# Casting weight loads, a state load in 512-byte runs, and an interleaved start, in an attention + FFN kernel

## The chip, the cores and the metric

One core of one Trainium2 chip. The metric is the device time of one execution in microseconds (us). A profile's "span" is from the first to the last instruction and is about 2 us shorter than the time. Engines: PE (matrix multiply), DVE (VectorE), ACT (ScalarE), POOL (GpSimd), SP (SyncE, which here only issues DMAs). A DMA "lands" when its data has arrived. To "evict" is to copy a result of PE out of its accumulator. The "granted clock" is the share of the full TensorE clock that the profile gives PE. Run to run the kernel before stays within 0.5% of its median.

## The reference, cut to what matters

```python
# x: (8, 8, 512, 64), state: (8, 8, 32, 64)  = batch, head, row, dim; fp32
scores = softmax(x @ state.T / 8)          # per batch and head: 512 x 32
xread  = scores @ state                    # 512 x 64
scores2 = softmax(state @ x.T / 8)         # 32 x 512
sread  = scores2 @ x                       # 32 x 64
tokens = concat([xread, sread], rows)      # (8, 544, 512), heads side by side
out = leaky_relu(tokens @ w_in) @ w_out    # w_in 512 x 2048, w_out 2048 x 512
```

Both kernels never form xread: since xread is A @ state, they compute M = state @ w_in per batch (called M below) and then FFN1 as A @ M. FFN1 is the product with w_in, FFN2 that with w_out. The largest piece is FFN2, 512 matmuls of 128x512 for the x rows alone.

## The kernel before

The loads and the order of the start are what the argument touches. Weights go through a staging tile of two buffers and are cast by DVE:

```python
    def load_w_in(n):
        st = stage.tile([P, NK, 512], FP32, name="w_stage", tag="w_stage", bufs=2)
        nc.sync.dma_start(st[:], moe_w_in[:, 512 * n:512 * (n + 1)].rearrange("(k p) c -> p k c", p=P))
        nc.vector.tensor_copy(w_in_bf[n][:], st[:])
    # ... load_w_out likewise
    def load_state():                       # eight DMAs, runs of 64 fp32 = 256 bytes
        for k in range(NK):
            for g in range(2):
                nc.scalar.dma_start(
                    stf[32 * k:32 * (k + 1), :, 64 * g:64 * (g + 1)],
                    state[:, 2 * k + g, :, :].rearrange("b n d -> n b d"))
    # ... cuts
    load_state(); load_x(0); load_w_in(0); load_x(1); load_w_in(1); load_x(2)   # lines joined here
    load_w_in(2); load_w_in(3)
    for n in range(4):
        load_w_out(n)
    prep_state()
    for b in range(AHEAD):                  # AHEAD = 2
        cast_x(b); att_xT(b, 0); att_xT(b, 1)
        att_scores(b); att_sread(b); att_aT(b)
    cast_x(2)
    for n in range(4):
        for b in range(AHEAD):
            m_chunk(b, n)
            for j in range(4 * n, 4 * n + 4):
                ffn1(b, j)
        # ... attention and M of batch 2
    for b in range(B):                      # steady state: FFN2 of b, FFN1 of b+2, attention of b+3
        # ...
```

The softmax here doesn't subtract the row's maximum and nothing guards it: scores larger than these inputs give would overflow.

Of the kernel before, what the change touches and what calls it, by code (L numbers as in the profile page):

```python
# [25 lines left out]
def kernel(  # L26
# [34 lines left out]
    stf = consts.tile([P, B, P], FP32, name="stf")  # L61
# [14 lines left out]

    def load_state():
        for k in range(NK):
            for g in range(2):
                nc.scalar.dma_start(  # L80
                    stf[32 * k:32 * (k + 1), :, 64 * g:64 * (g + 1)],
                    state[:, 2 * k + g, :, :].rearrange("b n d -> n b d"))

    def prep_state():
        for half in range(2):
            b0 = 4 * half
            nc.vector.tensor_copy(stb[:, b0:b0 + 4, :], stf[:, b0:b0 + 4, :])  # L87
            pst = psum.tile([P, 4, P], BF16, name="pst", tag="big")
            for i in range(4):
                nc.tensor.transpose(pst[:, i, :], stb[:, b0 + i, :], ident[:])  # L90
            for g in range(2):
                nc.vector.tensor_copy(  # L92
                    bd[64 * g:64 * (g + 1), b0:b0 + 4, :, g, :],
                    pst[64 * g:64 * (g + 1), :, :].rearrange("p b (k n) -> p b k n", k=NK),
                )

    def load_x(b):
        st = bt[b]
        st.xf = stage.tile([P, H, 4 * D], FP32, name="xf", tag="xf")
        nc.sync.dma_start(st.xf[:], x[b].rearrange("h (p t) d -> p h (t d)", t=4))  # L100

    def cast_x(b):
        st = bt[b]
        st.xb = attw.tile([P, 4, H, D], BF16, name="xb", tag="xb")
        for hh in range(2):
            src = st.xf[:, 4 * hh:4 * hh + 4, :].rearrange("p h (t d) -> p t h d", t=4)
            nc.gpsimd.tensor_copy(st.xb[:, :, 4 * hh:4 * hh + 4, :], src)  # L107

    def load_w_in(n):
        st = stage.tile([P, NK, 512], FP32, name="w_stage", tag="w_stage", bufs=2)  # L110
        nc.sync.dma_start(
            st[:], moe_w_in[:, 512 * n:512 * (n + 1)].rearrange("(k p) c -> p k c", p=P))
        nc.vector.tensor_copy(w_in_bf[n][:], st[:])

    def load_w_out(n):
        st = stage.tile([P, 4, DM], FP32, name="w_stage", tag="w_stage", bufs=2)
        nc.sync.dma_start(
            st[:], moe_w_out[512 * n:512 * (n + 1), :].rearrange("(j p) c -> p j c", p=P))
        nc.vector.tensor_copy(w_out_bf[n][:], st[:])


    def att_xT(b, half):
        st = bt[b]
        if half == 0:
            st.pxt = psum.tile([P, NK, 4, P], BF16, name="pxt", tag="big")
            st.xT = attw.tile([P, NK, 4, P], BF16, name="xT", tag="xT")
        for k in (2 * half, 2 * half + 1):
# [5 lines left out]
        if half == 1:  # L133
            nc.vector.tensor_copy(st.xT[:], st.pxt[:])  # L134

    def att_scores(b):
        st = bt[b]
        sc = psum.tile([P, 4, 2, NK, NS], FP32, name="sc", tag="big")
        for t in range(4):
            for k in range(NK):  # L140
                nc.tensor.matmul(  # L141
                    sc[:, t, :, k, :], lhsT=st.xT[:, k, t, :], rhs=bd[:, b, k, :, :],
                    start=True, stop=True)
        st.E = attw.tile([P, 4, 2, NK, NS], BF16, name="E", tag="E")
        nc.scalar.activation(out=st.E[:], in_=sc[:], func=ACTF.Exp, scale=SCALE)  # L145
        r1 = attw.tile([P, 32], FP32, name="r1", tag="r1")
        nc.vector.tensor_reduce(
            out=r1[:], in_=st.E[:].rearrange("p t g k n -> p (t g k) n"),
            op=ALU.add, axis=mybir.AxisListType.X)
        rr1 = attw.tile([P, 32], FP32, name="rr1", tag="rr1")  # L150
        nc.vector.reciprocal(rr1[:], r1[:])
        st.A = attw.tile([P, 4, 2, P], BF16, name="A", tag="A")
        nc.vector.tensor_tensor(  # L153
            out=st.A[:].rearrange("p t g (k n) -> p (t g k) n", n=NS),
            in0=st.E[:].rearrange("p t g k n -> p (t g k) n"),
            in1=rr1[:, :, None].to_broadcast([P, 32, NS]), op=ALU.mult)
# [24 lines left out]
    def att_aT(b):  # L181
        st = bt[b]
        pat = psum.tile([P, 2, 4, P], BF16, name="pat", tag="big")
        for g in range(2):
            for t in range(4):
                nc.tensor.transpose(pat[:, g, t, :], st.A[:, t, g, :], ident[:])  # L186
        st.aT = fpool.tile([P, 2, 4 * P], BF16, name="aT", tag="aT")
        nc.vector.tensor_copy(st.aT[:], pat[:].rearrange("p g t q -> p g (t q)"))  # L188


    def m_chunk(b, n):
# [10 lines left out]
        st.M[n] = fpool.tile([P, 2, 512], BF16, name=f"M{n}", tag=f"M{n}", bufs=2)  # L202
        nc.vector.tensor_copy(st.M[n][:], pm[:])
# [5 lines left out]
    def ffn1(b, j):  # L209
# [5 lines left out]
        for g in range(2):  # L215
            nc.tensor.matmul(  # L216
                ph[:], lhsT=st.M[n][:, g, P * jj:P * (jj + 1)], rhs=st.aT[:, g, :],
# [44 lines left out]
    load_state()  # L262
    load_x(0)
    load_w_in(0)
    load_x(1)
    load_w_in(1)
    load_x(2)
    load_w_in(2)
    load_w_in(3)
    for n in range(4):  # L270
        load_w_out(n)

    prep_state()
    for b in range(AHEAD):
        cast_x(b)
        att_xT(b, 0)
        att_xT(b, 1)
        att_scores(b)
# [80 lines left out]
```

## Time and profile before

| | before |
|---|---|
| time, median of 3 runs | 270.09 us (269.61 to 270.3) |
| span of the profile | 267.9 us |
| first FFN1 matmul | 47.8 us |
| first FFN2 matmul | 65.8 us |
| last matmul ends | 264.2 us |

The page of the kernel before: busy tenths in 40 slices of 6.7 us for PE and for the DMA engines, the GB/s moved per slice, and what was read from HBM.

```profile
PE   0015264999999999999999999999999999999994
...
DMA  7998999500023111111111111111111111122322
GB/s 212 324 348 300 337 379 364 166 0 2 1 76 123 42 39 42 39 39 57 49 48 47 39 42 39 42 39 39 42 39 39 42 39 39 42 78 80 78 81 78
...
HBM read 17.30 MB, written 8.91 MB: 98 GB/s over the span
```

PE has seven slices with little work and is then full to the end; the DMA engines are the opposite. The windows view cut at the first FFN1 and the first FFN2 gives the busy us (and instruction counts) of PE, PEld (weight load), DVE, ACT and POOL, then the granted PE clock, the DMA share and GB/s:

```profile
0.00:47.80 47.80, 13.66 (x153) 11.16 (x154) 24.61 (x34) 3.33 (x3) 10.94 (x15) 1.00 0.98 324
47.80:65.80 18.00, 17.92 (x97) 6.07 (x98) 7.22 (x6) 12.75 (x23) 0.00 (x0) 1.00 0.14 45
65.80:264.20 198.40, 197.69 (x1394) 96.37 (x1392) 91.26 (x107) 72.25 (x128) 8.55 (x8) 1.00 0.14 50
```

PE works 13.7 of the first 47.8 us and 215.6 of the 216.4 us after. So for a change that leaves PE's work as it is, the start is the only place to win time. The timeline of the kernel before (start, duration, engine, line, operation, what it waited for in brackets) shows why the start is long:

```profile
0.74 9.66 ACTq L80 DMA_DIRECT2D stf<-in_state_dram  x8
...
17.62 1.23 DVE L113 CAST w_in_bf_90<-w_stage 128x2048 bf16<-128x2048 f32 x1 [6.31 <-DMA w_stage<-in_moe_w_in_dram]
18.76 0.76 DVE L87 CAST stb<-stf 128x512 bf16<-128x512 f32 x2
...
30.86 1.23 DVE L119 CAST w_out_bf_93<-w_stage 128x2048 bf16<-128x2048 f32 x1 [1.18 <-DMA w_stage<-in_moe_w_out_dram]
32.01 1.22 DVE L153 TENSOR_TENSOR A<-E,rr_196 128x1024 bf16<-128x1024 bf16 x1
...
47.79 0.61 PE L216 MATMUL ph<-aT,M_339 128*128 128x512 bf16 x1 [0.51 <-DVE M_339 L203]
```

The ACT queue issues the state loads from 0.74 us for 9.66 us. The cast of state starts only at 18.76 us, behind a weight cast in DVE's order, and A, the normalised scores, stands behind the cast of a w_out chunk. A 1 MB weight chunk takes 7.7 to 9.9 us in the median from issue to landing, queued behind others, and a 64 KB piece of state 7.9 us.

### The profile page before, as it was taken

How to read it: one execution, taken by the hardware profiler on the slowest of the kernel's cores; microseconds unless marked ns; L12 is line 12 of the kernel's file. 1: busy time of each engine (PE TensorE's matmuls, PEld its weight loads, DVE VectorE, ACT ScalarE, POOL GpSimd, SP SyncE). 2: the span in 40 equal slices, each digit the busy share in tenths (PEclk: the TensorE clock that was granted, in tenths of full speed). 3: DMA queues.
4: the chain of work that ended last, by engine and by line, in shares of the span. 5: the costliest groups of instructions: out<-in, count | busy, mean ns of one | idle time of the engine just before them, and what ended most of it. 6: DMA issues, size and time to landing. Idle time of an engine off the chain costs nothing.

```text
span 267.9 us, 3811 instructions
## 1 busy us (share of the span) xinstructions
PE 229.3 (86%) x1640; PEld 113.6 (42%) x1640; DVE 123.8 (46%) x147; ACT 88.3 (33%) x153; POOL 19.5 (7%) x23
## 2 busy tenths in 40 slices
PE   0015264999999999999999999999999999999994
PEld 0014253224446435543554455455445555444441
DVE  0136869633787854745375456546542111222111
ACT  0101010577625333543443353434344444200000
POOL 3230303000030200300030000000000000000000
PEclk9999999999999999999999999999999999999999
DMA  7998999500023111111111111111111111122322
GB/s 212 324 348 300 337 379 364 166 0 2 1 76 123 42 39 42 39 39 57 49 48 47 39 42 39 42 39 39 42 39 39 42 39 39 42 78 80 78 81 78
DMA packets 19729, 26.46 MB, mean 99 GB/s; under 512 B 3073, under 2 KB 11265, under 8 KB 19713
## 3 DMA queue, kind: packets, MB, share of 16 engines
q1 hardware_dynamic: 17536, 25.69, 27.9%
q10 hardware_dynamic: 2176, 0.52, 0.9%
q8 instruction: 13, 0.21, 0.3%
q14 instruction: 4, 0.02, 0.0%
HBM read 17.30 MB, written 8.91 MB: 98 GB/s over the span
## 4 chain that ended last, share of the span: by engine, by line
PE 79%; DVE 9%; DMA 8%; ACT 1%; issue 1%; DVEq 0%; ACTq 0%
PE py L240 40%; PE ph L216 21%; PE pm L199 4%; DMA w_stage<-in_moe_w_in_dram 4%; PE pxt L129 3%; PE phs L225 3%; PE pys L252 3%; DMA xf<-in_x_dram 2%; DMA w_stage<-in_moe_w_out_dram 2%; DVE A L153 2%; PE pat L186 2%; PE sc L141 1%; ACT E L145 1%; DVE xT L134 1%; PE pr L168 1%; PE pr L162 1%
## 5 line engine op out<-in xcount | busy, mean ns | idle before, releaser
L207 ACT ACTIVATE hT<-ph 128x512 bf16<-128x512 f32 x128 | 75.0, 597 | 104.2 <-PE ph L216 104.2
L240 PEld LDWEIGHTS <-hT 128*128 128x128 bf16 x512 | 47.1, 98 | 51.6 <-issue 5.2
L245 DVE COPY ysb<-py 128x512 f32<-128x512 f32 x32 | 22.1, 692 | 61.2 <-PE py L240 61.2
L240 PE MATMUL py<-w_out_bf_95,hT 128*128 128x512 bf16 x128 | 33.5, 381 | 0.0
L240 PE MATMUL py<-w_out_bf_94,hT 128*128 128x512 bf16 x128 | 33.2, 380 | 0.0
L240 PE MATMUL py<-w_out_bf_93,hT 128*128 128x512 bf16 x128 | 33.2, 380 | 0.0
L240 PE MATMUL py<-w_out_bf_96,hT 128*128 128x512 bf16 x128 | 32.9, 380 | 0.0
L107 POOL CAST xb<-xf 128x1024 bf16<-128x1024 f32 x16 | 17.0, 1092 | 118.7 <-issue 55.2
L90 PE MATMUL pst<-ident,stb 128*128 128x128 bf16 x8 | 1.0, 311 | 19.2 <-DVE stb L87 19.2
L145 ACT ACTIVATE E<-sc 128x1024 bf16<-128x1024 f32 x8 | 8.2, 1023 | 27.2 <-PE sc L141 27.2
L134 DVE COPY xT<-pxt 128x2048 bf16<-128x2048 bf16 x8 | 9.8, 1225 | 15.3 <-PE pxt L129 15.3
L186 PE MATMUL pat<-ident,A 128*128 128x128 bf16 x64 | 5.7, 243 | 8.9 <-DVE A L153 8.9
L129 PE MATMUL pxt<-ident,xb 128*128 128x128 bf16 x128 | 12.1, 242 | 0.7 <-DVE bd L92 0.7
L129 PEld LDWEIGHTS <-xb 128*128 128x128 bf16 x128 | 9.9, 110 | 4.7 <-issue 1.4
L199 PEld LDWEIGHTS <-bd 64*32 64x32 bf16 x256 | 4.5, 90 | 16.8 <-issue 15.0
L186 PEld LDWEIGHTS <-A 128*128 128x128 bf16 x64 | 4.6, 108 | 10.6 <-DVE A L153 9.7
L90 PEld LDWEIGHTS <-stb 128*128 128x128 bf16 x8 | 0.8, 136 | 19.2 <-DVE stb L87 19.2
L188 DVE COPY aT<-pat 128x1024 bf16<-128x1024 bf16 x8 | 5.5, 682 | 7.2 <-PE pat L186 7.2
L141 PE MATMUL sc<-bd,xT 128*128 128x64 bf16 x128 | 5.8, 205 | 2.6 <-DVE xT L134 2.6
L162 PE MATMUL pr<-E,osel 128*128 128x128 bf16 x64 | 5.8, 241 | 2.3 <-ACT E L145 2.2
L141 PEld LDWEIGHTS <-xT 128*128 128x128 bf16 x128 | 5.2, 106 | 4.7 <-DVE xT L134 3.8
L162 PEld LDWEIGHTS <-osel 128*128 128x128 bf16 x64 | 5.0, 108 | 4.3 <-issue 2.8
(178 smaller groups left out, 254.2 us busy)
## 6 DMA issues: line engine op xcount, KB each, us to landing
xf<-in_x_dram SPq DMA_DIRECT2D x8, 1024.0 KB, 9.1
out_dram<-ysb SPq DMA_DIRECT2D x32, 256.0 KB, 2.3
w_stage<-in_moe_w_in_dram SPq DMA_DIRECT2D x4, 1024.0 KB, 9.9
w_stage<-in_moe_w_out_dram SPq DMA_DIRECT2D x4, 1024.0 KB, 7.7
stf<-in_state_dram ACTq DMA_DIRECT2D x8, 64.0 KB, 7.9
out_dram<-ysb SPq DMA_DIRECT2D x8, 64.0 KB, 1.7
```

Source lines behind the costliest of these rows:

```text
L107: nc.gpsimd.tensor_copy(st.xb[:, :, 4 * hh:4 * hh + 4, :], src)
L129: nc.tensor.transpose(st.pxt[:, k, t, :], st.xb[:, t, 2 * k:2 * k + 2, :].rearrange("p h d -> p (h d)"), ident[:])
L134: nc.vector.tensor_copy(st.xT[:], st.pxt[:])
L141: nc.tensor.matmul(sc[:, t, :, k, :], lhsT=st.xT[:, k, t, :], rhs=bd[:, b, k, :, :], start=True, stop=True)
L145: nc.scalar.activation(out=st.E[:], in_=sc[:], func=ACTF.Exp, scale=SCALE)
L162: nc.tensor.matmul(pr[:, 1, 0, :], lhsT=osel[:, g, :], rhs=st.E[:, t, g, :, :].rearrange("p k n -> p (k n)"), start=(i == 0), stop=(i == 7))
L186: nc.tensor.transpose(pat[:, g, t, :], st.A[:, t, g, :], ident[:])
L199: nc.tensor.matmul(pm[32 * k:32 * (k + 1), g, :], lhsT=bd[sl, b, k, g, :], rhs=w_in_bf[n][sl, k, :], start=True, stop=True)
L207: nc.scalar.activation(out=dst, in_=src, func=ACTF.Prelu, alpha=0.01)
L216: nc.tensor.matmul(ph[:], lhsT=st.M[n][:, g, P * jj:P * (jj + 1)], rhs=st.aT[:, g, :], start=(g == 0), stop=(g == 1))
L240: nc.tensor.matmul(acc.py[:], lhsT=st.hT[:, j, P * t:P * (t + 1)], rhs=w_out_bf[j // 4][:, j % 4, :], start=(j == 0), stop=(j == 15))
L245: nc.vector.tensor_copy(ysb[:], acc.py[:])
```

## The change

Its intent: take weight casts and staging off DVE by DMAs that cast while they move; load state in one DMA with runs of 512 bytes; and start FFN1 of batch 0 as soon as that batch is through attention, with everything else interleaved behind it. The Trainium skill, page "DMA: Bandwidth & Descriptors", section "SWDGE vs HWDGE vs iDMA", says that a DMA that casts has to be issued from GpSimd; that is why weights, and with them x of batches 1 and 2, move to that queue. The core of the diff:

```diff
 # weights: staging tile and VectorE cast replaced by a DMA that casts
     def load_w_in(n):
-        st = stage.tile([P, NK, 512], FP32, name="w_stage", tag="w_stage", bufs=2)
-        nc.sync.dma_start(
-            st[:], moe_w_in[:, 512 * n:512 * (n + 1)].rearrange("(k p) c -> p k c", p=P))
-        nc.vector.tensor_copy(w_in_bf[n][:], st[:])
+        nc.gpsimd.dma_start(
+            w_in_bf[n][:], moe_w_in[:, 512 * n:512 * (n + 1)].rearrange("(k p) c -> p k c", p=P))
 # ... load_w_out likewise

 # state: one load; a partition holds 512 contiguous bytes (two rows of one head) per batch
     def load_state():
-        for k in range(NK):
-            for g in range(2):
-                nc.scalar.dma_start(
-                    stf[32 * k:32 * (k + 1), :, 64 * g:64 * (g + 1)],
-                    state[:, 2 * k + g, :, :].rearrange("b n d -> n b d"))
+        stf = stage.tile([P, B, P], FP32, name="stf", tag="xf")
+        nc.sync.dma_start(
+            stf[:], state.rearrange("b h n d -> b (h n d)").rearrange("b (p c) -> p b c", p=P))
+        return stf
 # ... prep_state: 8 transposes become 32 small matmuls with columns of the identity

 # order of work (cut)
-    load_state()
-    load_x(0)
+    load_x(0, parts=2)
+    stf = load_state()
     load_w_in(0)
-    load_x(1)
+    load_x(1, nc.gpsimd)
     load_w_in(1)
-    load_x(2)
     load_w_in(2)
     load_w_in(3)
+    load_x(2, nc.gpsimd)
     for n in range(4):
         load_w_out(n)
-    prep_state()
-    for b in range(AHEAD):          # all of attention of 0 and 1 ...
-        cast_x(b)
-        att_xT(b, 0)
-        att_xT(b, 1)
-        att_scores(b)
-        att_sread(b)
-        att_aT(b)
-    # ... and only then state @ w_in (m_chunk) and FFN1 of 0 and 1
+    cast_x(0, ("dve", "act", "dve", "act"))
+    att_xT(0, 0, "dve")
+    att_xT(0, 1, "act")
+    prep_state(stf, 0, ("dve", "dve", "act"))
+    att_scores(0)
+    att_softmax(0, 2)
+    prep_state(stf, 1, ("dve", "dve", "act"))
+    m_early(0, 0, ("act", "act"))
+    att_aT(0, ("dve", "act"))
+    cast_x(1, ("dve", "act"))
+    m_early(1, 0, ("act", "act"))
+    att_xT(1, 0, "dve")
+    att_xT(1, 1, "dve")
+    m_early(0, 1, ("dve", "act"))
+    for j in range(4):
+        ffn1(0, j)
+    att_scores(1)
+    # ... FFN1 of 0 and 1 in groups of four, between them m_early of 0, 1 and 2,
+    #     attention of 1 and 2, and at the end att_sread(0) and att_sread(1)
```

Not shown in the cut: a first activation that loads ACT's table early, casts and copies spread over DVE and ACT, x of batch 0 in two halves, and more buffers for some tiles.

More of the change, by code (lines that the diff above doesn't have):

```diff
@@ L59 @@
     nc.gpsimd.memset(bd[:], 0.0)
-    stf = consts.tile([P, B, P], FP32, name="stf")
     stb = consts.tile([P, B, P], BF16, name="stb")
@@ L74 @@
     bt = [Batch() for _ in range(B)]
-    def load_state():
-        for k in range(NK):
-            for g in range(2):
-                nc.scalar.dma_start(
-                    stf[32 * k:32 * (k + 1), :, 64 * g:64 * (g + 1)],
-                    state[:, 2 * k + g, :, :].rearrange("b n d -> n b d"))
-    def prep_state():
-        for half in range(2):
-            b0 = 4 * half
-            nc.vector.tensor_copy(stb[:, b0:b0 + 4, :], stf[:, b0:b0 + 4, :])
-            pst = psum.tile([P, 4, P], BF16, name="pst", tag="big")
-            for i in range(4):
-                nc.tensor.transpose(pst[:, i, :], stb[:, b0 + i, :], ident[:])
-            for g in range(2):
-                nc.vector.tensor_copy(
-                    bd[64 * g:64 * (g + 1), b0:b0 + 4, :, g, :],
-                    pst[64 * g:64 * (g + 1), :, :].rearrange("p b (k n) -> p b k n", k=NK),
-                )
@@ L97, in load_x, with copy, prep_state @@
-    def load_x(b):
+    def copy(eng, dst, src):
+        if eng == "act":
+            nc.scalar.copy(dst, src)
+        elif eng == "pool":
+            nc.gpsimd.tensor_copy(dst, src)
+        else:
+            nc.vector.tensor_copy(dst, src)
+    def load_state():
+        stf = stage.tile([P, B, P], FP32, name="stf", tag="xf")
+        nc.sync.dma_start(
+            stf[:], state.rearrange("b h n d -> b (h n d)").rearrange("b (p c) -> p b c", p=P))
+        return stf
+    def prep_state(stf, half, engs):
+        bs = slice(4 * half, 4 * half + 4)
+        copy(engs[0], stb[:, bs, :], stf[:, bs, :])
+        pst = psum.tile([P, 4, NK, NS // 2, 2], FP32, name="pst", tag="ph")
+        sel = ident[:].rearrange("p (k g n) -> p k g n", k=NK, g=2)
+        for i in range(4):
+            for g in range(2):
+                for r in range(2):
+                    nc.tensor.matmul(
+                        pst[64 * g:64 * (g + 1), i, :, :, r],
+                        lhsT=stb[:, 4 * half + i, 64 * r:64 * (r + 1)], rhs=sel[:, :, g, :],
+                        start=True, stop=True)
+        for g in range(2):
+            sl = slice(64 * g, 64 * (g + 1))
+            copy(engs[1 + g], bd[sl, bs, :, g, :],
+                 pst[sl].rearrange("p b k n r -> p b k (n r)"))
@@ L98, in load_x @@
+    def load_x(b, eng=None, parts=1):
         st = bt[b]
         st.xf = stage.tile([P, H, 4 * D], FP32, name="xf", tag="xf")
-        nc.sync.dma_start(st.xf[:], x[b].rearrange("h (p t) d -> p h (t d)", t=4))
-    def cast_x(b):
-        st = bt[b]
-        st.xb = attw.tile([P, 4, H, D], BF16, name="xb", tag="xb")
-        for hh in range(2):
-            src = st.xf[:, 4 * hh:4 * hh + 4, :].rearrange("p h (t d) -> p t h d", t=4)
-            nc.gpsimd.tensor_copy(st.xb[:, :, 4 * hh:4 * hh + 4, :], src)
+        src = x[b].rearrange("h (p t) d -> p h (t d)", t=4)
+        w = H // parts
+        for i in range(parts):
+            hs = slice(w * i, w * (i + 1))
+            (eng or nc.sync).dma_start(st.xf[:, hs, :], src[:, hs, :])
@@ L109, in load_w_in, with cast_x @@
+    def cast_x(b, engs=("pool", "pool")):
+        st = bt[b]
+        st.xb = attw.tile([P, 4, H, D], BF16, name="xb", tag="xb", bufs=4)
+        w = H // len(engs)
+        for i, eng in enumerate(engs):
+            src = st.xf[:, w * i:w * (i + 1), :].rearrange("p h (t d) -> p t h d", t=4)
+            copy(eng, st.xb[:, :, w * i:w * (i + 1), :], src)
     def load_w_in(n):
-        st = stage.tile([P, NK, 512], FP32, name="w_stage", tag="w_stage", bufs=2)
-        nc.sync.dma_start(
-            st[:], moe_w_in[:, 512 * n:512 * (n + 1)].rearrange("(k p) c -> p k c", p=P))
@@ L113, in load_w_in @@
-        nc.vector.tensor_copy(w_in_bf[n][:], st[:])
+        nc.gpsimd.dma_start(
+            w_in_bf[n][:], moe_w_in[:, 512 * n:512 * (n + 1)].rearrange("(k p) c -> p k c", p=P))
     def load_w_out(n):
-        st = stage.tile([P, 4, DM], FP32, name="w_stage", tag="w_stage", bufs=2)
-        nc.sync.dma_start(
-            st[:], moe_w_out[512 * n:512 * (n + 1), :].rearrange("(j p) c -> p j c", p=P))
-        nc.vector.tensor_copy(w_out_bf[n][:], st[:])
-    def att_xT(b, half):
+        nc.gpsimd.dma_start(
+            w_out_bf[n][:], moe_w_out[512 * n:512 * (n + 1), :].rearrange("(j p) c -> p j c", p=P))
@@ L123, in att_xT @@
+    def att_xT(b, half, eng="dve"):
         st = bt[b]
@@ L126, in att_xT @@
             st.xT = attw.tile([P, NK, 4, P], BF16, name="xT", tag="xT")
+        ks = slice(2 * half, 2 * half + 2)
         for k in (2 * half, 2 * half + 1):
@@ L132, in att_xT @@
                     ident[:])
-        if half == 1:
-            nc.vector.tensor_copy(st.xT[:], st.pxt[:])
+        copy(eng, st.xT[:, ks, :, :], st.pxt[:, ks, :, :])
     def att_scores(b):
         st = bt[b]
-        sc = psum.tile([P, 4, 2, NK, NS], FP32, name="sc", tag="big")
+        st.sc = psum.tile([P, 4, 2, NK, NS], FP32, name="sc", tag="big")
         for t in range(4):
@@ L141, in att_scores, with att_softmax @@
                 nc.tensor.matmul(
-                    sc[:, t, :, k, :], lhsT=st.xT[:, k, t, :], rhs=bd[:, b, k, :, :],
+                    st.sc[:, t, :, k, :], lhsT=st.xT[:, k, t, :], rhs=bd[:, b, k, :, :],
                     start=True, stop=True)
-        st.E = attw.tile([P, 4, 2, NK, NS], BF16, name="E", tag="E")
-        nc.scalar.activation(out=st.E[:], in_=sc[:], func=ACTF.Exp, scale=SCALE)
-        r1 = attw.tile([P, 32], FP32, name="r1", tag="r1")
-        nc.vector.tensor_reduce(
-            out=r1[:], in_=st.E[:].rearrange("p t g k n -> p (t g k) n"),
-            op=ALU.add, axis=mybir.AxisListType.X)
-        rr1 = attw.tile([P, 32], FP32, name="rr1", tag="rr1")
-        nc.vector.reciprocal(rr1[:], r1[:])
-        st.A = attw.tile([P, 4, 2, P], BF16, name="A", tag="A")
-        nc.vector.tensor_tensor(
-            out=st.A[:].rearrange("p t g (k n) -> p (t g k) n", n=NS),
-            in0=st.E[:].rearrange("p t g k n -> p (t g k) n"),
-            in1=rr1[:, :, None].to_broadcast([P, 32, NS]), op=ALU.mult)
+    def att_softmax(b, parts=1):
+        st = bt[b]
+        st.E = attw.tile([P, 4, 2, NK, NS], BF16, name="E", tag="E", bufs=3)
+        st.A = attw.tile([P, 4, 2, P], BF16, name="A", tag="A")
+        r1 = attw.tile([P, 4, 8], FP32, name="r1", tag="r1")
+        rr1 = attw.tile([P, 4, 8], FP32, name="rr1", tag="rr1")
+        w = 4 // parts
+        for i in range(parts):
+            ts = slice(w * i, w * (i + 1))
+            nc.scalar.activation(out=st.E[:, ts], in_=st.sc[:, ts], func=ACTF.Exp, scale=SCALE)
+        for i in range(parts):
+            ts = slice(w * i, w * (i + 1))
+            Ev = st.E[:, ts].rearrange("p t g k n -> p (t g k) n")
+            rv = rr1[:, ts].rearrange("p t c -> p (t c)")
+            nc.vector.tensor_reduce(
+                out=r1[:, ts].rearrange("p t c -> p (t c)"), in_=Ev,
+                op=ALU.add, axis=mybir.AxisListType.X)
+            nc.vector.reciprocal(rv, r1[:, ts].rearrange("p t c -> p (t c)"))
+            nc.vector.tensor_tensor(
+                out=st.A[:, ts].rearrange("p t g (k n) -> p (t g k) n", n=NS),
+                in0=Ev, in1=rv[:, :, None].to_broadcast([P, 8 * w, NS]), op=ALU.mult)
     def att_sread(b):
@@ L179, in att_sread, with att_aT @@
                 in1=rr2[sl, :].rearrange("p (k n) -> p k n", n=NS), op=ALU.mult)
-    def att_aT(b):
+    def att_aT(b, engs=("dve",)):
         st = bt[b]
         pat = psum.tile([P, 2, 4, P], BF16, name="pat", tag="big")
-        for g in range(2):
-            for t in range(4):
-                nc.tensor.transpose(pat[:, g, t, :], st.A[:, t, g, :], ident[:])
-        st.aT = fpool.tile([P, 2, 4 * P], BF16, name="aT", tag="aT")
-        nc.vector.tensor_copy(st.aT[:], pat[:].rearrange("p g t q -> p g (t q)"))
+        st.aT = fpool.tile([P, 2, 4, P], BF16, name="aT", tag="aT")
+        w = 4 // len(engs)
+        for i, eng in enumerate(engs):
+            ts = slice(w * i, w * (i + 1))
+            for t in range(w * i, w * (i + 1)):
+                for g in range(2):
+                    nc.tensor.transpose(pat[:, g, t, :], st.A[:, t, g, :], ident[:])
+            copy(eng, st.aT[:, :, ts, :], pat[:, :, ts, :])
     def m_chunk(b, n):
@@ L201, in m_chunk, with m_early @@
                     rhs=w_in_bf[n][sl, k, :], start=True, stop=True)
-        st.M[n] = fpool.tile([P, 2, 512], BF16, name=f"M{n}", tag=f"M{n}", bufs=2)
-        nc.vector.tensor_copy(st.M[n][:], pm[:])
+        st.M[n] = fpool.tile([P, 2, 512], BF16, name=f"M{n}", tag=f"M{n}", bufs=3)
+        copy("dve", st.M[n][:], pm[:])
+    def m_early(b, n, engs=("act", "act")):
+        st = bt[b]
+        if n == 0:
+            st.M = [None] * 4
+        pm = [psum.tile([P, 512], FP32, name=f"pme{g}", tag="py") for g in range(2)]
+        for k in range(NK):
+            for g in range(2):
+                sl = slice(64 * g, 64 * (g + 1))
+                nc.tensor.matmul(
+                    pm[g][32 * k:32 * (k + 1), :], lhsT=bd[sl, b, k, g, :],
+                    rhs=w_in_bf[n][sl, k, :], start=True, stop=True)
+        st.M[n] = fpool.tile([P, 2, 512], BF16, name=f"M{n}", tag=f"M{n}", bufs=3)
+        for g in range(2):
+            copy(engs[g], st.M[n][:, g, :], pm[g][:])
     def lrelu(dst, src):
@@ L216, in ffn1 @@
             nc.tensor.matmul(
-                ph[:], lhsT=st.M[n][:, g, P * jj:P * (jj + 1)], rhs=st.aT[:, g, :],
+                ph[:], lhsT=st.M[n][:, g, P * jj:P * (jj + 1)], rhs=st.aT[:, g, :, :].rearrange("p t q -> p (t q)"),
                 start=(g == 0), stop=(g == 1))
@@ L259, in ffn2_s @@
             nc.sync.dma_start(out[r0:r0 + NS, :], ysb[NS * i:NS * (i + 1), :])
-    load_state()
-    load_x(0)
+    load_x(0, parts=2)
+    stf = load_state()
+    warm = consts.tile([P, 1], FP32, name="warm")
+    nc.vector.memset(warm[:], 0.0)
+    nc.scalar.activation(out=warm[:], in_=warm[:], func=ACTF.Exp)
     load_w_in(0)
-    load_x(1)
+    load_x(1, nc.gpsimd)
     load_w_in(1)
-    load_x(2)
     load_w_in(2)
     load_w_in(3)
+    load_x(2, nc.gpsimd)
     for n in range(4):
         load_w_out(n)
-    prep_state()
@@ L274 @@
-    for b in range(AHEAD):
-        cast_x(b)
-        att_xT(b, 0)
-        att_xT(b, 1)
-        att_scores(b)
-        att_sread(b)
-        att_aT(b)
-    cast_x(2)
-    for n in range(4):
-        for b in range(AHEAD):
-            m_chunk(b, n)
-            for j in range(4 * n, 4 * n + 4):
-                ffn1(b, j)
-        if n == 2:
-            att_xT(2, 0)
-            att_xT(2, 1)
-            att_scores(2)
-        if n == 3:
-            att_sread(2)
-            att_aT(2)
-            m_chunk(2, 0)
-            m_chunk(2, 1)
-            m_chunk(2, 2)
-            m_chunk(2, 3)
+    cast_x(0, ("dve", "act", "dve", "act"))
@@ new lines @@
+    att_xT(0, 0, "dve")
[14 more added lines that the diff above has]
+    att_scores(1)
+    att_softmax(1, 2)
+    m_early(2, 0, ("dve", "dve"))
@@ new lines @@
+    for j in range(4, 8):
+        ffn1(0, j)
+    m_early(1, 1, ("dve", "dve"))
+    m_early(0, 2, ("dve", "dve"))
+    for j in range(8, 12):
+        ffn1(0, j)
+    att_aT(1)
+    m_early(0, 3, ("dve", "dve"))
+    for j in range(12, 16):
+        ffn1(0, j)
+    cast_x(2, ("dve", "dve"))
+    m_early(2, 1, ("dve", "dve"))
+    for j in range(4):
+        ffn1(1, j)
+    att_xT(2, 0)
+    att_xT(2, 1)
+    m_early(1, 2, ("dve", "dve"))
+    for j in range(4, 8):
+        ffn1(1, j)
+    att_scores(2)
@@ L299 @@
+    att_softmax(2)
+    m_early(1, 3, ("dve", "dve"))
+    for j in range(8, 12):
+        ffn1(1, j)
+    att_sread(0)
+    m_early(2, 2, ("dve", "dve"))
+    att_aT(2)
+    for j in range(12, 16):
+        ffn1(1, j)
+    m_early(2, 3, ("dve", "dve"))
+    att_sread(1)
     for b in range(B):
@@ L308 @@
                 1: [lambda: att_xT(c, 1)],
-                3: [lambda: att_scores(c)],
+                3: [lambda: att_scores(c), lambda: att_softmax(c)],
                 5: [lambda: att_sread(c)],
+                2: [lambda: att_sread(2)] if b == 0 else [],
                 8: [lambda: att_aT(c)],
```

## The prediction

> **What bounds the kernel now.** The page's slices show two regimes: from about 48 us to the end the matmul engine (PE) is at 90% or more in every slice (granted clock 1.00), and the chain of waits is 79% PE. Before that PE does little: the timeline puts the first FFN1 matmul at 47.8 us and the first FFN2 matmul at 65.8 us, and the windows view gives PE 13.9 us of work in the first 48. In that front the DMA engines run at about 330 to 375 GB/s and the chain alternates between weight and x transfers (8 to 10 us for a queued 1 MB load) and VectorE (DVE), which has eight weight casts of 1.23 us in order before softmax steps. State is prepared only at 18.8 us, behind a cast that waited for w_in; A of batch 0 waits behind a cast of w_out (30.9 to 32.1 us).
>
> **What changes.** Removed: 9.8 us of DVE casts, staging waits, and state in 256-byte runs, issued on the ACT queue until 10.4 us. Added: weight loads as GpSimd DMAs that cast, batch 0 attention in smaller pieces over DVE and ACT, 32 small state matmuls for 8 transposes. Moved: FFN1 of batch 0 before attention of batches 1 and 2, sread of 0 and 1 behind it.
>
> **Cost.** PE work is hardly changed. From the first FFN1 to the last matmul the kernel before needs 216 us (47.8 to 264.2); the one after should need about 219, for attention of batch 1 and two sreads move into it (about 3 us net). So the gain is how much earlier dense PE work starts, less the stalls. I estimate x of batch 0 landed by 5.5 us, state by 7, scores at 12, softmax and aT by 17. In PE's order the first FFN1 stands behind a matmul on w_in chunk 1, which at 0.35 MB per us lands at 16 to 19 us. First FFN1: about 19 us, 29 earlier. Given back, estimated: x of batch 2 is behind all of w_in, while early loads of x 3 to 5 share the engines; it lands at 28 to 33 us, and its cast stands in DVE's order before M chunk 3 of batch 0, so PE stalls 2 to 5 us. Then DVE (M evictions at about 0.69 us per half, softmax) and ACT (0.60 us per FFN1 eviction) hold FFN1 back by 3 to 5 us. FFN2 starts near 48 us. Span near 19+219+7+4 (tail) = 249, and about 2 more as a time.
>
> **Prediction: 251 us, 8 in 10 within 244 to 261.** Faster by over 2%: 0.94; within 2%: 0.05; slower: 0.01.
>
> **What would show it.** The timeline: first FFN1 at 16 to 22 us, first FFN2 at 43 to 52. Slices: PE at 9 from there on, unchanged steady state. Waits in the front: PE on DVE and on casting DMAs (w_in chunk 1, x of batch 2). DVE without weight casts.
>
> **What would make it wrong.** The Trainium skill ("DMA: Bandwidth & Descriptors", SWDGE vs HWDGE vs iDMA) says that a cast in a DMA must be issued from GpSimd, whose cores write the descriptors, and the page "SBUF — State Buffer" (Who interferes with whom) that some DVE copies lock GpSimd out. No trace here shows such a DMA. If casting runs at half the read rate, w_out lands past 60 us and little is gained (265). If these transfers get the larger share against the SP queue, x of batch 2 comes earlier and it is 245.

## The result, and the profile after

The time is 249.06 us in the median (four runs, 247.61 to 252.03) against 270.12 us before (four runs; the 270.09 of the table is of three of them). The ratio is 0.920, with a 95% interval of 0.914 to 0.926. Ratios here are the mean time of one kernel's fast runs over that of the other's of the same rounds, so they are not quite the ratio of the medians quoted. The run of 252.03 us counts as slow, since it lies over 1.5% above the fastest of its kernel. A second set of six runs (label after_again, below), two of them slow (251.33 and 251.56 us), gave 248.14 us and 0.917.

The page of the kernel after, the same lines and that of the new queue (packets, MB, share of 16 engines), on which GpSimd issues:

```profile
PE   1086979999999999999999999999999999999994
...
DMA  6999999413111111111111111111111110121222
GB/s 214 268 225 305 266 246 263 161 35 136 46 42 42 45 42 45 42 42 45 42 42 45 42 42 45 42 45 42 42 42 45 42 42 14 73 84 61 69 86 84
...
q0 software_dynamic: 4768, 6.29, 12.4%
...
HBM read 17.30 MB, written 8.91 MB: 105 GB/s over the span
```

Two things need care. The bytes read from HBM are the same, 17.30 MB: a casting DMA reads all of fp32, and the GB/s row counts the bf16 bytes that it writes: 6.29 MB on the new queue are 8 MiB of fp32 weights counted as half, and 2 MiB of x. And the DMA engines are busy for as long as before, about eight slices; the whole gain is in PE's row. The windows of the kernel after, cut at its first FFN1, its first FFN2 and the last matmul:

```profile
0.00:24.10 24.10, 9.25 (x104) 6.16 (x105) 8.79 (x20) 10.07 (x16) 10.30 (x17) 0.96 1.03 249
24.10:55.90 31.80, 29.66 (x261) 13.25 (x259) 23.40 (x38) 19.49 (x35) 5.08 (x5) 0.98 0.83 198
55.90:244.70 188.80, 188.80 (x1303) 93.11 (x1301) 82.10 (x105) 66.32 (x117) 6.20 (x6) 1.00 0.14 51
```

The first FFN1 comes at 24.1 us instead of 47.8, 23.7 us earlier. From there to the last matmul it takes 220.8 us (24.14 to 244.93), 4.4 us more than the 216.4 before, since part of attention now lies in that stretch. PE is idle for 2.1 us between the first FFN1 and the first FFN2 (31.8 less 29.7) and not at all afterwards. The granted clock of 0.96 and 0.98 comes of one stretch at 0.50, from 22.0 to 25.4 us, across the first FFN1; 1.3 us of it lie in the dense part. The timeline of the kernel after:

```profile
1.77 0.50 SPq L87 DMA_DIRECT2D stf<-in_state_dram  x1
...
12.73 1.00 DVE L82 CAST stb<-stf 128x512 bf16<-128x512 f32 x2 [6.24 <-DMA stf<-in_state_dram]
...
21.97 0.61 PE L239 MATMUL pme_273<-w_in_bf_89,bd 64*32 64x512 bf16 x4
...
24.14 1.66 PE L257 MATMUL ph<-aT,M_222 128*128 128x512 bf16 x4
...
30.10 1.74 DVE L176 TENSOR_TENSOR A<-E,rr_323 128x512 bf16<-128x512 bf16 x2
...
35.35 0.68 DVE L82 CAST xb<-xf 128x1024 bf16<-128x1024 f32 x1
```

State is issued at 1.77 us and its cast starts at 12.73 us. The matmul on w_in chunk 1 (the tile pme at 21.97) and the first FFN1 follow. The cast of x of batch 2 at 35.35 us waits for nothing. The chain of waits of the kernel after (start, duration, what) begins with that landing and goes on through attention to the first FFN1:

```profile
1.77 10.94 DMA stf<-in_state_dram
...
12.73 0.69 DVE stb L82
...
24.32 1.48 PE ph L257 x4
```

So the state load, 10.94 us, is the longest single link of the start, and the prediction had it landing at 7 us.

### The profile page after: what moved, and what is told of

The parts are those of the page before. It is cut to its first block, busy times and chain, and to the rows that moved or that the text cites. A ratio compares the mean times of both kernels' runs of the same rounds, so it can differ in the third digit from the quotient of the medians.

```text
span 248.6 us, 3872 instructions
## 1 busy us (share of the span) xinstructions
PE 227.9 (92%) x1664; PEld 112.5 (45%) x1664; DVE 115.0 (46%) x163; ACT 95.9 (39%) x168; POOL 21.6 (9%) x27
## 3 DMA queue, kind: packets, MB, share of 16 engines
q0 software_dynamic: 4768, 6.29, 12.4%
HBM read 17.30 MB, written 8.91 MB: 105 GB/s over the span
## 4 chain that ended last, share of the span: by engine, by line
PE 86%; DVE 5%; DMA 4%; ACT 2%; SPq 0%; issue 0%
PE py L281 45%; PE ph L257 21%; DMA stf<-in_state_dram 4%; PE pxt L143 3%; PE phs L266 3%; PE pys L293 3%; PE pm L224 3%; PE pat L212 2%; DVE A L176 1%; PE pr L190 1%; PE pr L184 1%; PE sc L154 1%; ACT hT L248 1%; PE pst L99 1%; ACT E L167 1%; DVE M_342 L82 1%
## 5 line engine op out<-in xcount | busy, mean ns | idle before, releaser
L143 PE MATMUL pxt<-ident,xb 128*128 128x128 bf16 x128 | 11.9, 236 | 5.1 <-DVE xb L82 5.1
L82 DVE COPY xT<-pxt 128x1024 bf16<-128x1024 bf16 x15 | 10.4, 691 | 10.8 <-PE pxt L143 10.8
L80 POOL CAST xb<-xf 128x1024 bf16<-128x1024 f32 x10 | 11.3, 1154 | 41.8 <-PE pr L190 23.6
L143 PEld LDWEIGHTS <-xb 128*128 128x128 bf16 x128 | 9.4, 106 | 9.1 <-DVE xb L82 5.0
L99 PE MATMUL pst<-ident,stb 128*64 128x64 bf16 x32 | 2.4, 342 | 7.4 <-DVE stb L82 7.4
L82 DVE COPY aT<-pat 128x1024 bf16<-128x1024 bf16 (+1 forms) x8 | 5.2, 654 | 7.4 <-PE pat L212 7.4
L167 ACT ACTIVATE E<-sc 128x1024 bf16<-128x1024 f32 (+1 forms) x10 | 8.3, 853 | 0.0
L248 ACT ACTIVATE hTs<-phs 128x256 bf16<-128x256 f32 x16 | 6.1, 378 | 0.0
L212 PEld LDWEIGHTS <-A 128*128 128x128 bf16 x64 | 4.1, 100 | 4.2 <-DVE A L176 2.6
L99 PEld LDWEIGHTS <-stb 128*64 128x64 bf16 x32 | 1.7, 186 | 7.9 <-DVE stb L82 7.6
## 6 DMA issues: line engine op xcount, KB each, us to landing
stf<-in_state_dram SPq DMA_DIRECT2D x1, 512.0 KB, 10.9
w_in_bf_89<-in_moe_w_in_dram POOLq DMA_DIRECT2D x1, 512.0 KB, 12.6
```

The lines of the kernel that those rows point to most:

```text
L80: nc.gpsimd.tensor_copy(dst, src)
L82: nc.vector.tensor_copy(dst, src)
L143: nc.tensor.transpose(st.pxt[:, k, t, :], st.xb[:, t, 2 * k:2 * k + 2, :].rearrange("p h d -> p (h d)"), ident[:])
L167: nc.scalar.activation(out=st.E[:, ts], in_=st.sc[:, ts], func=ACTF.Exp, scale=SCALE)
L212: nc.tensor.transpose(pat[:, g, t, :], st.A[:, t, g, :], ident[:])
L248: nc.scalar.activation(out=dst, in_=src, func=ACTF.Prelu, alpha=0.01)
```

## The experiments

Every variant starts from the kernel after unless it says "on the kernel before". The start is summed up by three numbers that the timeline gives: when the cast of state starts, when the first FFN1 starts, and how long it is from there to the end of the span. The tile framework orders the instructions of each engine anew for each variant, so an edit can shift neighbours a little.

### 1. Is the late state a matter of sharing or of short runs?

**hold**: no casting DMA is issued before state has landed.

```diff
+    hold = consts.tile([P, 1], FP32, name="hold")
+    nc.gpsimd.tensor_copy(hold[:], stf[:, 0, 0:1])
     load_w_in(0)
```

> The kernel after with one tiny GpSimd copy that reads the state tile ahead of the first weight load, so that no casting DMA is issued before state has landed. In the kernel after, state took 10.9 us from issue to landing (12.7 us on the clock of the span). Theory 1 (the state packets of 512 bytes share the DMA engines with the casting DMAs and get the small share): state lands by 6 to 8 us, the cast of state starts there, and the first FFN1 matmul comes at 18 to 22 us instead of 24.1, unless w_in chunk 1, now issued 4 us later, takes its place as the last wait (it then lands near 18 to 20). Time 244 to 249. Theory 2 (512-byte runs are slow by themselves): state still lands at 11 to 13 us, all weights come 9 us later, the first FFN1 is at 29 us or later, time 252 to 256.

Measured: 252.31 us, ratio 0.932 (0.930 to 0.934). State landed 5.8 us after its issue, by 7.6 us, as theory 1 says; but the first FFN1 came at 26.2 us and the time was worse. That the time lies in the range of theory 2 has other reasons. The timeline of hold:

```profile
7.61 0.76 DVE L82 CAST stb<-stf 128x512 bf16<-128x512 f32 x2 [1.35 <-DMA stf<-in_state_dram]
...
16.40 0.63 PE L239 MATMUL pme<-w_in_bf,bd 64*32 64x512 bf16 x8 [4.82 <-DMA w_in_bf<-in_moe_w_in_dram]
...
20.42 3.72 DVE L176 TENSOR_TENSOR A<-E,rr 128x512 bf16<-128x512 bf16 x2
20.95 2.03 POOL L80 CAST xb<-xf 128x1024 bf16<-128x1024 f32 x2
...
26.15 0.63 PE L257 MATMUL ph<-aT,M 128*128 128x512 bf16 x1
```

Two new waits took the place of the old one. PE waited 4.82 us for w_in chunk 0, which now landed at 16.4 us and stands in PE's order before most of the score matmuls. And A took 3.72 us for two pieces (1.28 us in the kernel after; one of the two took 3.12 us here) while a POOL cast of 2.03 us ran beside it. The Trainium skill, page "SBUF — State Buffer", section "Who interferes with whom", says that a DVE instruction with two SBUF inputs contends with a GpSimd instruction that reads SBUF; this agrees, for A reads E and the reciprocals. The kernel after has the same collision for batch 1, milder: A at 30.10 us took 1.74 us. So theory 1 was right about the landing, and its expected time was a miss: the weights were held back as well, and A met the POOL cast.

**state_act**: state gets the ACT queue, its own, and the weights are issued as in the kernel after.

```diff
-        nc.sync.dma_start(
+        nc.scalar.dma_start(
             stf[:], state.rearrange(...))
```

> The kernel after with the state load issued on the ACT queue instead of behind the two halves of x on the SP queue; weights are issued as before. Theory 1 (sharing with the casting DMAs): state gets a queue of its own from 0.8 us, most of it moves before the first casting DMA is issued at 3.0 us, it lands at 6 to 9 us, the first FFN1 is 2 to 4 us earlier (20 to 22 us), time 245 to 248. Theory 2 (512-byte runs slow by themselves): it lands no earlier than 10 us, time 248 to 250. x of batch 0 should land up to 1.5 us later in both.

Measured: 247.10 us (245.82 to 248.95), ratio 0.916 (0.910 to 0.921). The timeline of state_act:

```profile
6.87 0.76 DVE L82 CAST stb<-stf 128x512 bf16<-128x512 f32 x2 [0.98 <-DMA stf<-in_state_dram]
...
17.74 0.63 PE L239 MATMUL pme<-w_in_bf,bd 64*32 64x512 bf16 x8 [1.10 <-DMA w_in_bf<-in_moe_w_in_dram]
...
19.59 0.59 PE L257 MATMUL ph<-aT,M 128*128 128x512 bf16 x1
...
26.78 3.08 DVE L82 CAST M<-pme 128x512 bf16<-128x512 f32 x5
...
30.69 0.69 DVE L82 CAST xb<-xf 128x1024 bf16<-128x1024 f32 x1 [0.23 <-DMA xf<-in_x_dram]
```

State landed by 6.9 us and the first FFN1 started at 19.59 us, with w_in issued as before (w_out 1 us later), so short runs are not slow by themselves. But the edit does two things: state has its own queue, and it is issued 1 us earlier, 2.2 us ahead of the first casting DMA. Which of them helped is not tested. The second half of x of batch 0 pays: its casts start at 8.12 us instead of 5.89. The Trainium skill ("DMA: Bandwidth & Descriptors", "Queues, rings and completion order") says that each DMA engine takes turns between queues packet by packet, a packet being a group of descriptors. That a queue of small packets gets few bytes per turn beside one of larger packets is a guess from this; no run here shows the turns. The landing times agree with it only in part: 5.8 us with nothing issued behind state (hold), 10.9 us in the kernel after, but 6.8 us beside the same kind of casting DMAs in cast_state_again and 7.8 us without any in no_cast (both below). From the first FFN1 to the end of the span it is 224.0 us, as in the kernel after (224.5). Whether the 5 us between the two profiles are worth as much in the median, these runs don't say: the intervals of the ratios overlap, and the next run shows why.

**after_again**: the kernel after, unchanged, with five rounds and a second profile.

> The kernel after once more, for its median on this chip and a second look at its profile: 247.5 to 250.5 us; state landing at 11 to 14 us and first FFN1 at 22 to 26 us, if the late state is its habit and not one execution's accident.

Measured: 248.14 us (247.25 to 251.56), ratio 0.917 (0.915 to 0.920). The profile missed both expectations for the start. Its timeline:

```profile
9.40 0.76 DVE L82 CAST stb<-stf 128x512 bf16<-128x512 f32 x2 [2.91 <-DMA stf<-in_state_dram]
...
21.00 1.45 PE L257 MATMUL ph<-aT,M 128*128 128x512 bf16 x3
```

Two of the six runs are slow; the four fast ones lie between 247.25 and 248.81 us. The same kernel had state 3.3 us earlier than in its first profile, the first FFN1 3.1 us earlier, and a span of 245.6 instead of 248.6 us. Landing beside the casting DMAs varies from execution to execution (7.6 and 10.9 us), and in these two the span follows it one for one. With two profiles this is a possible cause of the wider spread of the kernel after, not a shown one; both profiled runs count as fast, and no slow one was profiled. The clock adds to the doubt: it was granted at 0.50 from 16.8 to 23.6 us here and from 22.0 to 25.4 in the first profile.

### 2. Which part of the change earns the gain?

Every subset of the three parts was run: C (casting DMAs), S (the new state load), O (the new order of work). Each part is a bundle. S takes eight DMAs of 256-byte runs off the ACT queue, puts one of 512-byte runs behind x of batch 0 on the SP queue, and replaces the transposes; what the run length alone is worth was not tested. O is all the rest of the diff.

**cast_only** (C on the kernel before):

```diff
-        nc.sync.dma_start(st[:], moe_w_in[...])      # and the staging tile
-        nc.vector.tensor_copy(w_in_bf[n][:], st[:])
+        nc.gpsimd.dma_start(w_in_bf[n][:], moe_w_in[...])   # w_out likewise
```

> The kernel before with the casting DMAs alone (no staging tile, no weight casts on VectorE); state load and order of work as before. If the casting DMAs carry most of the gain of 21 us: time 253 to 259, first FFN1 at 32 to 37 us, x of batches 1 and 2 landing much earlier since the SP queue is free of weights. If the order of work carries most of it: 263 to 268.

Measured: 270.34 us, ratio 0.999 (0.996 to 1.001). Both guesses missed: nothing was gained. The chain of waits of cast_only:

```profile
8.57 13.84 DMA stf<-in_state_dram
...
22.59 0.44 DVE stb L87
...
46.99 1.49 PE ph L212 x3
```

State, in its 256-byte form, was complete only at 22.4 us; the cast began at 22.59 us, 3.8 us later than before. The first FFN1 followed 24.4 us after that, where the kernel before needs 29.0 us (18.76 to 47.79). What the casts give is eaten by the state that they delay.

**state_only** (S on the kernel before; load_state and prep_state of the kernel after, all copies on DVE):

> The kernel before with the new state load and its preparation alone. State lands by 8 to 10 us, but attention of batches 0 and 1 still runs in full before the first FFN1 and VectorE still has the weight casts in between: first FFN1 at 42 to 47 us, time 264 to 269. If state was the whole wait of the front: 258 to 262.

Measured: 259.92 us, ratio 0.961 (0.958 to 0.963). That is the range of the second guess, but state was not the whole wait. The cast of state started at 8.37 us, the first FFN1 at 37.39 us: again 29.0 us later. The chain of waits shows the weight casts still in it:

```profile
24.45 1.23 DVE w_in_bf L124
...
34.97 1.23 DVE w_out_bf L130
...
37.39 1.03 PE ph L227 x2
```

**cast_state** (C and S on the kernel before):

> Casting DMAs and new state load together, in the order of work of before. In the run with the casting DMAs alone the first FFN1 came 24.4 us after state (22.6 to 47.0). If it is state that holds the casting DMAs' gain back: state at 11 to 14 us, first FFN1 at 35 to 38 us, time 257 to 261. If the old order needs the time anyway: 266 to 270.

Measured: 256.89 us in the median of all four runs, ratio of the three fast ones 0.948 (0.943 to 0.952); the fast runs are 254.70 to 257.22. The first execution, the one that was profiled, took 603 us. It is a slow run and no part of any comparison; it is told of under the last heading. The kernel was profiled once more:

> The kernel with casting DMAs and new state load in the old order once more, because the profiled execution of its first run took 603 us with PE slow throughout and its trace is of no use for times. Expected span about 253 to 256, first FFN1 at 33 to 37 us, 220 us from there to the end, as in the three other kernels of the old order.

Measured, one run: 254.83 us; cast of state at 8.06 us, first FFN1 at 31.84 us, 221.2 us from there to the end of the span. Here is when state was there:

```profile
8.06 1.22 DVE L82 CAST stb<-stf 128x512 bf16<-128x512 f32 x2 [6.80 <-DMA stf<-in_state_dram]
```

State and the first FFN1 came earlier than both expectations (11 to 14 us for state; 35 to 38, then 33 to 37 for FFN1). State landed 6.8 us after its issue although casting DMAs were issued from 2.96 us on; so they alone do not make it late. From state to FFN1 it is 23.8 us, as in cast_only (24.4) and against 29.0 without C. So the casting DMAs do take about 5 us off that chain; how much of it shows in the time depends on when state comes.

**no_cast** (S and O; weights back through the SP queue and DVE casts; two output tiles instead of three, to make room for the staging tiles):

```diff
-        nc.gpsimd.dma_start(w_in_bf[n][:], moe_w_in[...])
+        st = stage.tile([P, NK, 512], FP32, name="w_stage", tag="w_stage", bufs=2)
+        nc.sync.dma_start(st[:], moe_w_in[...])
+        nc.vector.tensor_copy(w_in_bf[n][:], st[:])         # w_out likewise
-    load_x(1, nc.gpsimd)
+    load_x(1)                                               # x of 2 likewise
```

> The kernel after with only the casting DMAs undone: weights through the SP queue into two staging tiles and cast on VectorE, as before (x of batches 1 and 2 on the SP queue too, two output tiles instead of three to make room). If the casting DMAs carry most of the gain: 261 to 268, with eight casts of 1.23 us in VectorE's order and PE waiting for them between 15 and 50 us. If the order of work carries it: 250 to 255. State should land by 7 to 9 us here, since w_in chunk 0 stands behind it on the same queue: that is a further test of theory 1.

Measured: 257.97 us, ratio 0.954 (0.951 to 0.956), between the two guesses. The first FFN1 is at 24.75 us, only 0.6 us later than in the kernel after's first profile, but from there to the end of the span it takes 231.0 us instead of 224.5. The chain of waits of no_cast:

```profile
32.04 5.33 DMA w_stage<-in_moe_w_out_dram
...
37.40 1.23 DVE w_out_bf L136
38.62 0.61 DVE M L82
...
39.28 1.03 PE ph L261 x2
```

DVE waits for a w_out chunk, casts it, and only then evicts the M tile that FFN1 needs. PE starts early and then runs into the staged weights: it is idle for 6.1 us between the first FFN1 and the first FFN2, 4 us more than in the kernel after. Then comes something else. The row of the granted clock on the page of no_cast (slices of 6.4 us), and two pieces of its chain, each of two FFN1 matmuls:

```profile
PEclk9999995799999999999999999999999999999999
...
40.85 0.97 PE ph L261 x2
...
49.39 0.45 PE ph L261 x2
```

From 37.7 to 48.0 us, right behind the idling, the clock was 0.50 and FFN1 went at half its later pace. PE was busy 8.7 us of that stretch, so it cost up to some 4 us (an estimate: half of the 8.7, if PE had met no other wait). Waits and clock together are what the longer rest is made of. The four runs of no_cast have mean clocks of 0.973 to 0.980, so it is no accident of one execution; whether the idling brought the low clock about, no run here tests. State took 7.8 us to land here (its cast began at 9.55 us, a little later than expected), with weights behind it on its own queue: casting DMAs are not the only traffic that slows it, but no run without them showed 10.9 us for this load.

**old_state** (C and O; eight 256-byte-run loads on the ACT queue and transposes with the identity):

> The kernel after with only the state part undone: eight loads in 256-byte runs on the ACT queue and transposes with the identity, casting DMAs and new order kept. If small packets starve beside the casting DMAs, as the run with the casting DMAs alone suggests (state complete at 22.4 us there, time unchanged), state is complete at 20 to 24 us here, the first FFN1 comes at 30 to 35 us, time 255 to 260. If the state load's form does not matter once the order is changed: 248 to 251.

Measured: 252.96 us, ratio 0.936 (0.934 to 0.938), between the two guesses. The cast of state started at 16.0 us, not 20 to 24, and the first FFN1 at 27.8 us. In this variant the GpSimd queue waited 10.0 us for a tile that state had to free, so fewer loads ran beside state than in cast_only; the landing is therefore not a clean measure of the 256-byte form.

**order_only** (O: old state load, staged weights):

> The new order of work alone: old state load and staged weights with VectorE casts. If order is worth about the same with and without the other parts: state at 16 to 19 us, first FFN1 at 28 to 32 us, time 260 to 264. If order is worth nothing without early state: 267 to 270.

It has two output tiles instead of three, as no_cast. Measured: 258.01 us, ratio 0.957 (0.952 to 0.961), better than expected. Cast of state at 19.2 us, first FFN1 at 31.1 us.

All eight, with the ratio to the kernel before of the same rounds. The last three columns are from the profiles, one execution each (two for the last row), in us; "rest" is the span less the start of the first FFN1.

| parts | run | time, us | ratio | cast of state | first FFN1 | rest |
|---|---|---|---|---|---|---|
| none | before | 270.1 | 1 | 18.8 | 47.8 | 220.1 |
| C | cast_only | 270.3 | 0.999 | 22.6 | 47.0 | 220.3 |
| S | state_only | 259.9 | 0.961 | 8.4 | 37.4 | 220.4 |
| C S | cast_state, cast_state_again | 256.6 (fast runs) | 0.948 | 8.1 | 31.8 | 221.2 |
| O | order_only | 258.0 | 0.957 | 19.2 | 31.1 | 225.2 |
| C O | old_state | 253.0 | 0.936 | 16.0 | 27.8 | 223.0 |
| S O | no_cast | 258.0 | 0.954 | 9.6 | 24.8 | 231.0 |
| C S O | after, after_again | 249.1, 248.1 | 0.920, 0.917 | 12.7, 9.4 | 24.1, 21.0 | 224.5, 224.6 |

The parts do not add up. In the old order the rest is the same within 1.1 us whatever the loads do, and the time follows the first FFN1 alone. The new order brings FFN1 nearer to state (without C from 29.0 us to 11.9 in O and 15.2 in S O; with C from about 24 to under 12) and pays 3 to 11 us in the rest, least with C. S adds nothing to O alone (0.954 and 0.957, overlapping intervals), because what it wins at the start is lost again in the rest, to waits for staged weights and the stretch at half clock; it adds about 4 us to C and O (253.0 to 249.1). C alone adds nothing, but with S and O it is worth about 9 us (258.0 to 249.1), of which up to some 4 us are that stretch at half clock, by the estimate above.

### 3. Can the late state and the eviction chain be had back?

In state_act, DVE evicts five M pieces one after another from 26.78 us, and ACT is idle meanwhile. **split_evict** is state_act with three of these evictions on ACT:

```diff
-    m_early(1, 1, ("dve", "dve"))
+    m_early(1, 1, ("dve", "act"))      # and (0, 2), (0, 3)
```

> State on the ACT queue (as in the run state_act, where VectorE evicted M tiles one after another from 26.8 to 29.9 us while PE waited 0.2 us for each and ACT idled 3.7 us), and three of those evictions given to ACT. If that chain on VectorE is the last wait there: 1 to 2 us less than state_act, 244.5 to 246.5 us in the median. If x of batch 2 (landed 30.7 us there) is the wait right behind it, nothing is gained: 246 to 248.

**late_x** is split_evict with x of batches 3 and 4 issued behind the last weights:

```diff
     for n in range(4):
         load_w_out(n)
+    load_x(3, nc.gpsimd)
+    load_x(4, nc.gpsimd)
 # and in the loop:
-            load_x(c)
+            if c > 4:
+                load_x(c)
```

> The same, and x of batches 3 and 4 issued on the GpSimd queue behind the last weights instead of early on the SP queue. Weights and x of batch 2 then share the engines with nothing from about 8 us: w_in chunk 1 should land 2 us earlier than in state_act (17.7 us), x of batch 2 by 24 to 26 us, first FFN1 at 18 to 19 us, and PE meets no DMA wait after. Time 243 to 246, 1 to 2 us below split_evict if DMA waits still cost it; equal if not. A loss would mean that the casts of x 3 now come too late for batch 3.

Measured, in the same call as after_again (248.14 us, 0.917, 0.915 to 0.920): split_evict 246.01 us, ratio 0.911 (0.908 to 0.913); late_x 245.40 us, ratio 0.908 (0.906 to 0.911). One run of split_evict is slow (249.56). Both beat both kernels: their intervals lie below that of the kernel after, late_x by about 1%. Between these two the intervals overlap, and split_evict was not run beside state_act, so what the split evictions earn by themselves stays open. The timeline of late_x:

```profile
16.51 0.76 PE L239 MATMUL pme<-w_in_bf,bd 64*32 64x512 bf16 x8
...
18.66 1.91 PE L257 MATMUL ph<-aT,M 128*128 128x512 bf16 x4
...
28.74 1.28 DVE L82 CAST xb<-xf 128x1024 bf16<-128x1024 f32 x2
```

The matmul on w_in chunk 1 no longer waits (17.74 us, after 1.10 us of waiting, in state_act), the first FFN1 starts at 18.66 us, and the cast of x of batch 2 starts at 28.74 us without a wait (x landed at 24.6). But the rest is now 225.0 us (243.7 less 18.7). The chain of late_x begins with the second half of x of batch 0, which landed at 8.0 us, and goes on through attention to FFN1: with state early, that load is the first wait.

## Why the prediction was right or wrong

The predicted 251 us (244 to 261) holds the measured 249.06 us, and the mechanism held: the start is shortened, PE is full behind it, and the steady state is unchanged. But two of its terms were off by some 5 us each in the profiled execution, in opposite directions: FFN1 came 5.1 us late, and the 7 us of stalls were 2.1. That the number came so close is partly luck.

- **"State by 7"** failed. State was there at 12.7 us in one profile and 9.4 us in another. The prediction moved weights to a second queue; that these may get the larger share it named only as a help to x of batch 2, not as a delay of state. hold shows that the bulk loads beside it can cost state time: 5.8 us from issue to landing with none issued, 7.6 and 10.9 us with them. They need not: it was 6.8 us in cast_state_again. What made one execution take 10.9 us stays open. Issued first and on a queue of its own it took 6.0 to 6.1 us (state_act, split_evict, late_x).
- **"First FFN1: about 19 us"** was therefore 24.1 (21.0 in the second profile). From state to FFN1 the prediction had 12 us; it was 11.4 and 11.6. The w_in chunk named as its last wait landed at 17.3 us (issued 4.73, 12.6 us to landing), within the predicted 16 to 19, and was not what held it. It became the last wait once state was early: 1.10 us in state_act.
- **"PE stalls 2 to 5 us" for x of batch 2** did not happen. It landed at 28.9 us (issued 7.04, 21.9 us to landing), within the predicted 28 to 33, but DVE reached its cast only at 35.35 us. Even with FFN1 at 19.6 us, in state_act, that wait was 0.23 us. The place of the cast in DVE's order was right and the time at which DVE gets there was wrong.
- **"DVE and ACT hold FFN1 back by 3 to 5 us"** was too much: PE's idle time between first FFN1 and first FFN2 is 2.1 us in all. The prediction summed for that stretch 219 + 7 us to the last matmul; it was 220.8 us, of which PE was busy for 218.5 and idle for about 2. So the work was sized rightly and the stalls were not.
- **"FFN2 starts near 48"** was 55.9 us, outside its 43 to 52. It started 5 us late with FFN1 and had more in front of it than allowed for, but that is work that is then done, so it cost nothing at the end.
- **"Removed: 9.8 us of DVE casts"** has no term of its own in the prediction's sum, rightly so. It gains nothing by itself (cast_only, 0.999) and about 9 us with the rest (no_cast against after, the clock included).
- **The doubt about casting at half the read rate** did not come true. All weights had landed by 46.9 us (the last issued 15.23, 31.7 us to landing), not past 60, with the same bytes read from HBM.

## What to carry to other kernels

Before you put bulk loads on a second DMA queue, look which small load the first matmul waits for, and issue it first, on a queue where nothing stands ahead of it; here a 512 KB load took 6.0 to 6.1 us so, in three kernels, and 6.8 to 10.9 us behind x of batch 0 with casting DMAs beside it. Cut the start at the first matmul of the dense phase, and read "when does it start" and "how long from there" separately: a part that moves one of them can be eaten by the other, and parts that each look worthless or sufficient alone can need each other. An estimate that comes out right may hold two errors of opposite sign, and only the marks in the profile that it named show that.

## What the Trainium skill lacked or had wrong

- "DMA: Bandwidth & Descriptors" states turns by packet between queues, but gives no size for what that does to a small load beside casting DMAs: 512 KB of state in 512-byte runs landed after 5.8 us with no bulk load beside it, after 7.1 and 7.8 us with staged weights (state_only, no_cast), and after 6.8 (cast_state_again), 7.6 and 10.9 us (two executions of one kernel) with casting DMAs; in 256-byte runs over eight DMAs it was complete only at 22.4 us.
- The same page has no rate for DMAs that cast. Here w_out chunks of 1 MB of fp32 landed at 33.0, 37.3, 41.5 and 46.9 us, 4.2 to 5.4 us apart, with x loads on the SP queue beside them. On issuing, one of its tables ("Anatomy of one DMA — SWDGE (gpsimd) path") calls descriptor generation small, another ("Latency and other measured facts") gives this path a first byte after about 1 us because of it; here each DMA issued from POOL took 0.74 to 0.91 us of that engine, ten of them between 2.96 and 15.97 us, which fits the second.
- "TensorE: Matmul & The Clock Gate" ("Wait — 56ns, not 53.3ns?") gives about 107 ns for a cold and 56 ns for a warm 128-column matmul, and the runs agree: 16 transposes at 20.95 us in the kernel before, just after PE's long idling, take 1.87 us (104 ns from start to start, as the last alone takes 0.31), and 8 at 56.8 us in the kernel after take 0.45 us of its chain of waits (56 ns each). The profile's granted clock is 1.00 in both places. In the trace of the kernel before, the clock's record begins only at 50.9 us, and 1.00 is what the views print where there is none. So 1.00 there does not rule out a cold start; a printed 0.50, as in no_cast, went with half pace.
- The same page ("Seeing it yourself") warns that a trace's clock events can be unreliable and that the clock has been seen stuck at a quarter for over 50 us. One execution, the first of cast_state, was slow on PE for its whole 601.6 us: 128x512 matmuls took 828 ns in the mean instead of 380, while ACT's evictions took their usual 597 ns each. Its granted clock is printed as 1.0, but its trace holds no record of the clock at all; so whether the clock was low stays open. The next three runs of the same kernel were normal. The line of its FFN2 matmuls in the groups view (busy us, mean ns, idle before):

```profile
L247 PE MATMUL py<-w_out_bf,hT 128*128 128x512 bf16 x512 | 324.8, 828 | 0.0
```
